# A long-convolution and token-MLP kernel: 16-bit table angles, three filter blocks evacuated by VectorE, the first filter half by column halves

## Chip, cores and metric

The kernel runs on one core of one Trainium2 chip. The metric is the device time of one execution in microseconds (us). Eleven runs of the kernel before had a median of 181.88 us (181.64 to 182.03). Names of engines in the profile are PE (TensorE), PEld (TensorE's weight loads), DVE (VectorE), ACT (ScalarE), POOL (GpSimd) and SP (SyncE, which only issues transfers here).

## The reference

Two branches of a mixer are computed on the same input and blended by a gate. Branch A convolves along the sequence (2048 positions, 640 channels) with a filter as long as the sequence; branch B is a layer norm and a two-layer MLP over the tokens.

```
x = A_q                                           # (1, 2048, 640)
g = sigmoid((x * gate_w).sum(-1))
# branch A
k_shift = sum over t<4 of k delayed by t, times shift_k
kv      = k_shift * v
y       = irfft(rfft(kv padded to 4096) * rfft(ssm_k padded to 4096))[:2048]
a       = x * (y + kv * ssm_D)
# branch B
h = layernorm(x)
u = gelu(einsum("bsd,sf->bdf", h, w1) + b1)       # w1: 2048 x 1536
b = (einsum("bdf,fs->bds", u, w2) + b2).transpose # w2: 1536 x 2048
out = g * a + (1 - g) * b
```

## The kernel before

**The work.** The convolution is done with transforms written as matmuls. A table FTB holds cosines and sines for four residues p = 0 to 3 of the position modulo 4 (128 partitions x 1024 values for each p). VectorE makes integer angles (`pint`), masks them to 4095, and ScalarE takes the sine of each block ("sin" in the source, `FTB<-pint,cst` in the profile). The filter `ssm_k` arrives with channels on partitions; TensorE transposes it by matmuls against an identity, in two halves h of the sequence and five blocks db of 128 channels (`transp`), and the transposed blocks are copied from PSUM to `wT`. The transforms of the filter (`fwd` for half 0, `fwd_even` and `fwd` for half 1, named "W") multiply `wT` by the table; ScalarE copies each result from PSUM to `C` ("We"). VectorE then mixes the four residues into spectra. The same is done for kv, the spectra are multiplied on VectorE, and the inverse transform runs on TensorE again. The MLP (`X`, `ring`, `GT`, `W2`) fills TensorE in between: matmuls "m1" of the first layer use the normalized `X`, those of the second layer, "m2", follow. VectorE takes the layer norm's statistics tile by tile (`ln_tile`, sixteen tiles of 128x640), POOL raises the variance to the power -0.5 (`ln_scale`, tile `rstd`), and VectorE normalizes in place (`ln_apply`), eight tiles at a time.

**Small parts at the start.** `zz` is a tile of zeros; TensorE multiplies it by itself in a few "spin" matmuls ahead of each transposed block of half 0 (`SPIN = (7, 3, 3, 2, 2)`). `ident` is the identity, made by VectorE out of POOL's `dif`. `rows` holds small constants that are rearranged by a VectorE copy ("taps") and transposed on TensorE into `cw`; POOL expands `cw` and the mask `m32` into `KF`, the weights of the four-tap shift. ssm_D is added to the filter's tap 0: its one row `Drow` is folded into the first transpose of every block of half 0 by an extra one-row matmul.

**What sets the order.** Every engine runs its instructions in the order in which they were issued. That order comes from a planner inside the kernel (`_Sched`), which at build time plays the instructions through with assumed costs (the second argument of `SC.add`, `dve_dur`, `act_dur`, or a `.dur` set by hand), picks the ready instruction with the smallest priority, and hands out four PSUM slots of two banks each (`pp0` to `pp3`; at most two to the MLP and three to the rest). A tracker (`_Tracker`) then adds the waits that data and buffers need. Planned times are only the planner's: on the chip the order is fixed, and the waits hold. Nearly all instructions are emitted by helpers, so one line of the profile stands for many: L295 is every matmul, L670 every ScalarE operation, L626 every `tensor_tensor`, L640 and L641 every `tensor_scalar`, L922 and L926 the statistics, L264 the transfers that add into their target, issued by POOL.

**Transfers.** SP issues the loads in program order: ssm blocks 0 and 1 to 2, then X's first quarter, then ssm blocks 3 to 4, the rest of X, biases, the second filter half, then w1, k and more.

Of the kernel before, what the change touches and what calls it, by code (L numbers as in the profile page):

```python
# [9 lines left out]
BF16 = mybir.dt.bfloat16  # L10
F32 = mybir.dt.float32
I32 = mybir.dt.int32
ACT = mybir.ActivationFunctionType
ALU = mybir.AluOpType

# [3 lines left out]
class _Tracker:  # L19
# [31 lines left out]
    def regions(self, ap):  # L51
        name = ap.tensor.name
        info = self.mem.get(name)
        if info is None:
            return []
        space, base, rowsize, esize = info
        apl = [tuple(p) for p in ap.ap]
        esz_ap = mybir.dt.size(ap.dtype)
        assert esz_ap == esize, "bitcast size change unsupported in tracker"
        off = ap.offset  # L60
        assert isinstance(off, int)
        pstride, pcount = apl[0]
        if pcount > 1:
            assert pstride == rowsize, (name, apl, rowsize)
        p0 = off // rowsize
        rem = off % rowsize
        p1 = p0 + pcount
        assert p1 <= 128
        free = apl[1:]
        outer = free[:-1]  # L70
        inner = free[-1:] if free else []
        nouter = 1
        for st, ct in outer:
            nouter *= ct
        res = []
        if outer and nouter <= 64:
            idxs = [0] * len(outer)
            for _ in range(nouter):
                o = rem
                for (st, ct), i in zip(outer, idxs):  # L80
                    o += st * i
                lo = o
                hi = o
                for st, ct in inner:
                    ext = st * (ct - 1)
                    if ext < 0:
                        lo += ext
                    else:
                        hi += ext
                hi += 1  # L90
                assert lo >= 0 and hi <= rowsize, (name, apl, off, rowsize)
                res.append(self._reg(space, p0, p1, base + lo * esize, base + hi * esize))
                for d in range(len(outer) - 1, -1, -1):
                    idxs[d] += 1
                    if idxs[d] < outer[d][1]:
                        break
                    idxs[d] = 0
        else:
            lo = rem
            hi = rem  # L100
            for st, ct in free:
                ext = st * (ct - 1)
                if ext < 0:
                    lo += ext
                else:
                    hi += ext
            hi += 1
            assert lo >= 0 and hi <= rowsize, (name, apl, off, rowsize)
            res.append(self._reg(space, p0, p1, base + lo * esize, base + hi * esize))
        return res  # L110
# [172 lines left out]
    def mm(self, ps_ap, lhsT, rhs, start, stop, final_val, inc, transpose=False):  # L283
# [8 lines left out]
                acc.append((r, "W"))  # L292
        need = self.deps_for("PE", acc)
        self.do_waits("PE", need)
        ins = self.nc.tensor.matmul(ps_ap, lhsT=lhsT, rhs=rhs, start=start, stop=stop, skip_group_check=True)  # L295
        src = ("eng", "PE", final_val)
        for reg, mode in acc_r:
            self.add_record(reg, "R", src)
# [213 lines left out]
def _build(nc, A_q, A_k, A_v, A_shift_k, A_ssm_k, A_ssm_D, B_x, B_w1, B_b1, B_w2, B_b2, gate_w, out):  # L512
# [6 lines left out]
    SL = 4 * D  # L519
# [3 lines left out]
    with ExitStack() as es:  # L523
# [58 lines left out]
        C = [alloc(f"C{i}", [128, 4, 4, D], BF16) for i in range(4)]  # L582
        SS = alloc("SS", [128, 2, 4, D], BF16)
        E_base = cur[0]
        acol = alloc("acol", [128, 2, 4], I32, at=base_of(SS))
        brow = alloc("brow", [128, 2, 128], I32, at=base_of(SS) + 64)
        dif = alloc("dif", [128, 128], I32, at=base_of(SS) + 64 + 1024)
        dif2 = alloc("dif2", [128, 32], I32, at=base_of(SS) + 64 + 1536)
        KT = [alloc(f"KT{i}", [128, NG, KTW], BF16) for i in range(2)]
# [4 lines left out]
        v1 = alloc("v1", [128, 2, 4, D], BF16, at=base_of(C[3]) + 2 * SL * 2)  # L594
        kv1 = alloc("kv1", [128, 2, 4, D], BF16, at=E_base)
        ksh = [alloc(f"ksh{i}", [128, 4, D], BF16, at=base_of(GT) + 5120 * (1 + i)) for i in range(2)]
        rows = alloc("rows", [20, 5, 512], BF16, at=base_of(GT))
        kn = [alloc(f"kn{i}", [128, 4, D], BF16, at=base_of(ring[1]) + 5120 * i) for i in range(2)]
        kp = [alloc("kp0", [128, NG, 128], BF16, at=base_of(ring[1]) + 10240), alloc("kp1", [128, NG, 128], BF16, at=base_of(GTB))]
        pint = alloc("pint", [128, 4, 2, 2, 256], I32, at=base_of(ring[1]))  # L600
        W2 = alloc("W2", [128, 32, 512], BF16, at=base_of(ring[0]))
        assert base_of(ring[1]) == base_of(ring[0]) + 16384
        O1 = alloc("O1", [128, 4, 4, D], BF16, at=base_of(X))
# [161 lines left out]

        SSM0 = ((0, 1), (1, 3), (3, 5))
        SSM1 = ((0, 2), (2, 5))
        small(Drow[:, :], dr(A_ssm_D, 0, [[0, 1], [1, D]]), 1280, "QA")
        small(rows[0:20, 0, 0:128], dr(A_shift_k, 0, [[128, 20], [1, 128]]), 5120, "QA")
        for a, b in SSM0[:2]:  # L770
            ssm_load(0, a, b)
        x_load(0)
        ssm_load(0, *SSM0[2])
        for hk in range(1, 4):
            x_load(hk)
        small(rows[0:4, 1, :], dr(B_b2, 0, [[512, 4], [1, 512]]), 4096, "SP", chain=True)
# [8 lines left out]
        SPIN = (7, 3, 3, 2, 2)  # L785

        def spin(k):
            return [((lambda s: s[:, 0:512]), zz[:, 0:128], zz[:, :], True, True)] * k

        T_PI = float(np.float32(math.pi * (1.0 - 1e-6)))  # L790
        memset("DVE", cst[:, 0:1], T_PI)
        memset("DVE", cst[:, 1:2], -0.5)
        iota = lambda ap, pat, b, cm: SC.add("POOL", 0.2, lambda s: T.op("POOL", lambda e: e.iota(ap, pat, base=b, channel_multiplier=cm), [], [ap]), [], [ap])
        iota(dif[:, :], [[1, 128]], 0, -1)
        iota(acol[:, :, :], [[4, 2], [1, 4]], 0, 8)
        iota(brow[:, :, :], [[-512, 2], [4, 128]], 1, 0)
        iota(dif2[:, :], [[1, 32]], 128, -1)
        ts("DVE", ident[:, :], dif[:, :], 0.0, None, ALU.is_equal)
        memset("POOL", rows[0:20, 3:5, :].rearrange("g a b -> g (a b)")[:, 0:896], 0.0)
        ro, ri = V(rows, 1536, [[128, 4], [160, 4], [1, 32]], pn=20), V(rows, 0, [[1, 4], [0, 4], [4, 32]], pn=20)  # L800
        SC.add("DVE", 0.6, lambda s: T.op("DVE", lambda e: e.tensor_copy(ro, ri), [ri], [ro]), [ri], [ro], prio=0, name="taps")
        PORD = (0, 2, 1, 3)
        sins = {}
        for p in PORD:
            pv = pint[:, p, :, 1, :]
            t_ = tt("DVE", pv, V(acol, p, [[4, 2], [0, 256]]), V(brow, 0, [[0, 2], [1, 256]]), ALU.mult, mode=1)
            ts("DVE", pint[:, p, :, 0, :], pv, 1024.0, None, ALU.add, mode=2)
            pa = pint[:, p, :, :, :].rearrange("q a b c -> q (a b c)")
            if p != 0:
                t_.after.add(pprev)  # L810
            pprev = ts("DVE", pa, pa, 4095, None, ALU.bitwise_and, mode=2)
            pv3 = pa
            sins[p] = act(FTB[:, p, :, :, :, :].rearrange("q a b c d -> q (a b c d)"), pa, ACT.Sin, bias=cst[:, 0:1],
                scale=-(2.0 * math.pi / 4096.0) * (1.0 - 1e-6), name="sin")

        for hk in range(2):
            k_load(hk)
# [14 lines left out]
        def consts():  # L832
# [5 lines left out]
            mms(vt, items, name="cst")  # L838
            act(cc[:, :], lambda s: s[:, 0:28], ACT.Copy, vt=vt, name="cc")

        def transp(h, db):
            vt = _VT("cv")
            items = []
            for kt in range(2):
                for p in range(4):
                    o = (lambda s, j=4 * kt + p: s[:, 128 * j:128 * j + 128])
                    dfold = h == 0 and kt == 0 and p == 0
                    if dfold:
                        items.append((o, ident[0:1, :], Drow[0:1, 128 * db:128 * db + 128], True, False))
                    items.append((o, V(ssm, db * S + 1024 * h + 4 * kt + p, [[8, 128]]), ident[:, :], not dfold, True))  # L850
            m_ = mms(vt, (spin(SPIN[db]) if h == 0 else []) + items, name="wtr")
            m_.dur = 0.5
            o_ = act(V(wT, 2 * h * SL + 128 * db, [[SL, 2], [D, 4], [1, 128]]), (lambda s: s[:, :].rearrange("q (a b c) -> q a b c", a=2, b=4)), ACT.Copy, vt=vt, name="wT")
            if h == 0:
                o_.after.add(sins[0 if db == 0 else 2])

        def fwd(src, h, p, dst, slot, scale, name, neg=lambda c, k2: False):
            for k2 in range(2):
# [80 lines left out]
                o_.after.update(lnlast[-1:])  # L939

        MIXP = 330
        LNA = 8
        lnlast = []
        kfirst = []
        KFP = (0, 5, 10, 15)
        srcW = lambda h: (lambda kt, p, ci: wT[:, 2 * h + kt, p, 320 * ci:320 * ci + 320])
        for h in range(2):
            for db in range(ND):
# [2 lines left out]
                consts()  # L951
            if h in (1,):
                fwd_even(srcW(h), h, C[h], 1.0 / 1024.0, h == 1, "W")
            for p in (PORD if h not in (1,) else PORD[2:]):
                if h == 0 and p in (1, 3):
                    sins[p].prio = SC.ops[-1].idx - (16.5 if p == 1 else 8.5)
                fwd(srcW(h), h, p, C[h], p, 1.0 / 1024.0, "W", (lambda c, k2: False) if h == 0 else (lambda c, k2: c == 1))
            if h == 0:
                for t in range(8):
# [11 lines left out]
                ln_apply(LNA, 16)  # L971
                lnlast.append(SC.ops[-1])
                for g0 in KFP:
                    tt("POOL", KF[:, g0:g0 + 20 // len(KFP), :, :], V(cw, 7 * g0, [[7, 20 // len(KFP)], [1, 7], [0, 32]]), V(m32, 0, [[0, 20 // len(KFP)], [0, 7], [1, 32]]), ALU.mult, xr=[pv3] if g0 == 0 else []).after.update(kfirst[:1])
                    kfirst.append(SC.ops[-1])
                for hk in range(2):
                    k_turn(hk)
# [341 lines left out]
```

## Time and profile before

| what | value |
|---|---|
| median of 11 runs | 181.88 us (181.64 to 182.03) |
| the profiled execution | 181.97 us, of which the profile's span covers 180.1 us |
| PE busy | 173.9 us, 97% of the span |
| DVE busy | 171.3 us, 95% |
| ACT busy | 117.0 us, 65% |
| POOL busy | 43.7 us, 24% |
| chain that ended last | PE 88%, ACT 10% |
| mean DMA rate | 242 GB/s |

The page gives the busy share of each engine, and the chain that ended last says which of them decided in each stretch. Spin matmuls on `zz` count as busy PE, so that the busy share of PE contains them. A start time is counted from the first instruction of the profile. Two instructions in a row on one engine can overlap by some tens of nanoseconds, so durations add up to a little more than the time they take together.

### The profile page before, as it was taken

The page shows a single profiled execution, that of the slowest core. Times are in us where ns is not written, and L with a number is a line of the kernel's source. Part 1 is how long each engine was busy: PE and PEld are TensorE (multiplying, and loading weights), DVE is VectorE, ACT ScalarE, POOL GpSimd, SP SyncE. Part 2 cuts the span into 40 slices and gives each one's busy share as a digit, 9 for nine tenths or more (in the row PEclk, how much of TensorE's full clock was granted, in tenths as well). Part 3 has the DMA queues.
Part 4 walks back from the last instruction along what each step waited for, and adds up shares of the span by engine and source line. Part 5 has one row for each costly group of instructions (what it writes and reads, how often), then busy time and mean ns, then how long its engine had stood idle before and what let it go on. Part 6 is the DMA issues. An engine that isn't in the chain of part 4 may idle for free.

```text
span 180.1 us, 3335 instructions
## 1 busy us (share of the span) xinstructions
PE 173.9 (97%) x1381; PEld 129.2 (72%) x1381; DVE 171.3 (95%) x203; ACT 117.0 (65%) x176; POOL 43.7 (24%) x42
## 2 busy tenths in 40 slices
PE   7979998989999999999999999999999999999994
PEld 2646785577779677776677778888888887777772
DVE  7999895999999999999999899999999999999984
ACT  5798998899898999616999933132131223753760
POOL 4079504090000054100240110402626000252000
PEclk9999999999999999999999999999999999999999
DMA  5999999999999999998399969798899999599563
GB/s 152 371 411 374 386 292 188 236 420 338 202 255 299 187 277 251 237 219 197 56 240 305 203 80 361 181 214 273 155 196 218 207 201 380 225 151 241 118 228 140
DMA packets 38543, 43.51 MB, mean 242 GB/s; under 512 B 15868, under 2 KB 31361, under 8 KB 38529
## 3 DMA queue, kind: packets, MB, share of 16 engines
q1 hardware_dynamic: 33296, 32.16, 58.1%
q0 software_dynamic: 5200, 11.14, 35.5%
q8 instruction: 11, 0.18, 0.4%
q14 instruction: 4, 0.02, 0.0%
q10 hardware_dynamic: 32, 0.01, 0.0%
HBM read 25.87 MB, written 2.62 MB: 158 GB/s over the span
## 4 chain that ended last, share of the span: by engine, by line
PE 88%; ACT 10%; DVE 0%; issue 0%
PE pp L295 88%; ACT wT L670 3%; ACT C L670 2%; ACT ksh L670 2%; ACT FTB L670 2%; ACT L670 1%; ACT GT L670 0%; DVE O L682 0%; DVE zz L686 0%; ACT cw L670 0%; DVE cst L686 0%
## 5 line engine op out<-in xcount | busy, mean ns | idle before, releaser
L295 PE MATMUL pp<-X,ring 128*128 128x320 bf16 x384 | 55.6, 299 | 0.0
L626 DVE TENSOR_TENSOR C<-C 128x2560 bf16<-128x2560 bf16 (+2 forms) x37 | 54.5, 1522 | 0.0
L295 PE MATMUL pp<-GT,W 128*128 128x320 bf16 x384 | 52.6, 299 | 0.0
L295 PEld LDWEIGHTS pp<-GT,W 128*128 128x128 bf16 x384 | 43.6, 114 | 8.6
L295 PEld LDWEIGHTS pp<-X,ring 128*128 128x128 bf16 x384 | 37.2, 98 | 14.7 <-DVE X L641 0.4
L670 ACT ACTIVATE C<-pp 128x640 bf16<-128x640 f32 x64 | 40.4, 723 | 4.8 <-PE pp L295 4.8
L670 ACT ACTIVATE O<-pp,c,omg 128x640 bf16<-128x640 f32 x15 | 13.3, 885 | 34.7 <-PE pp L295 34.7
L264 POOL DMA_DIRECT2D C<-C x8 | 10.9, 1611 | 41.7 <-DVE C L626 38.3
L295 PE MATMUL pp<-wT,FTB 128*128 128x320 bf16 x112 | 17.2, 299 | 2.1 <-ACT wT L670 1.0
L670 ACT ACTIVATE cgb<-pp,gg 128x640 bf16<-128x640 f32 x16 | 12.7, 794 | 5.7 <-PE pp L295 5.3
L295 PEld LDWEIGHTS pp<-wT,FTB 128*128 128x128 bf16 x112 | 10.5, 98 | 7.4 <-ACT wT L670 1.5
L670 ACT ACTIVATE GT<-pp,cc 128x640 bf16<-128x640 f32 x12 | 9.6, 800 | 9.0 <-PE pp L295 9.0
L626 DVE TENSOR_TENSOR tm<-C,C 128x2560 bf16<-128x2560 bf16 (+1 forms) x7 | 14.3, 2057 | 0.0
L922 DVE BATCH_NORM_STATS2 stats<-X 128x6 f32<-128x320 bf16 x32 | 13.6, 462 | 0.3 <-DMA X<-in_A_q_dram 0.3
L295 PE MATMUL pp<-C,FTB 128*128 128x320 bf16 x96 | 13.4, 299 | 0.0
L264 POOL DMA_DIRECT2D C<-q_hi x6 | 5.9, 977 | 27.7 <-DVE C L626 13.2
L295 PEld LDWEIGHTS pp<-C,FTB 128*128 128x128 bf16 x96 | 9.3, 98 | 3.8 <-issue 0.2
L670 ACT ACTIVATE gq<-gq 128x640 bf16<-128x640 bf16 x16 | 11.8, 741 | 0.0
L626 DVE TENSOR_TENSOR SS<-C 128x2560 bf16<-128x2560 bf16 x8 | 11.7, 1489 | 0.1
L626 DVE TENSOR_TENSOR C<-tm 128x2560 bf16<-128x2560 bf16 (+1 forms) x9 | 10.7, 1193 | 0.1
L670 ACT ACTIVATE wT<-pp 128x1024 bf16<-128x1024 f32 x10 | 9.7, 1040 | 1.0 <-PE pp L295 1.0
L670 ACT ACTIVATE ksh<-pp 128x1024 bf16<-128x1024 f32 (+1 forms) x12 | 9.8, 894 | 0.6 <-PE pp L295 0.6
(73 smaller groups left out, 194.8 us busy)
## 6 DMA issues: line engine op xcount, KB each, us to landing
ring<-in_B_w_dram SPq DMA_DIRECT2D x12, 512.0 KB, 7.7
W<-in_B_w_dram SPq DMA_DIRECT2D x12, 512.0 KB, 6.4
C<-C POOLq DMA_DIRECT2D x8, 640.0 KB, 10.6
X<-in_A_q_dram SPq DMA_DIRECT2D x4, 640.0 KB, 8.9
kn<-in_A_k_dram SPq DMA_DIRECT2D x4, 640.0 KB, 9.4
out_dram<-O SPq DMA_DIRECT2D x7, 320.0 KB, 3.4
C<-SS POOLq DMA_DIRECT2D x3, 640.0 KB, 11.7
ssm<-in_A_ssm_k_dram SPq DMA_DIRECT2D x3, 512.0 KB, 7.3
```

What stands on the lines that cost most here:

```text
L264: ins = engobj.dma_start(out_ap, in_ap, accum_op=ALU.add, max_dma_last_dim=2560)
L295: ins = self.nc.tensor.matmul(ps_ap, lhsT=lhsT, rhs=rhs, start=start, stop=stop, skip_group_check=True)
L626: o_ = SC.add(eng, d, lambda s: T.op(eng, lambda e: e.tensor_tensor(o, a, b, op), rd, [o]), rd, [o], prio=prio, name="tt")
L670: return T.op("ACT", lambda e: e.activation(o, src, func, **kw), rr + [src], ww)
L922: ops.append(SC.add("DVE", 0.38, (lambda o, i: lambda s: T.op("DVE", lambda e: e.bn_stats(o, i), [i], [o]))(o, i), [i], [o]))
```

## The change

Five things are changed together.

1. **Angles in 16 bits.** One 128x128 product of partition and column index, masked to 4095, is kept as a 16-bit table `tb` (with its copy shifted by 1024). POOL writes eight 16-bit rows `jrow` of offsets. Each block's angles are one 16-bit sum of the two and one 16-bit mask, in place of a 32-bit product, a 32-bit sum over half the block and a 32-bit mask. `pint` shrinks to 16 bits.
2. **Transposes in bf16.** The transposes write bf16 into PSUM (`is_transpose`), 2 KB for each block instead of 4 KB, and the spin matmuls write into the slot's other bank. Blocks 0 to 2 of half 0 are copied to `wT` by VectorE (`evac_dve`), the rest by ScalarE as before.
3. **ssm_D by columns.** ssm_D is loaded as five rows of 128, transposed once by TensorE (`dcol`), copied by VectorE to `Dc` and added into the loaded filter by three small VectorE operations (`addD`). The one-row matmuls go.
4. **The first filter half by column halves.** `fwd_c` runs all four residues for columns 0 to 319, which need blocks 0 to 2, and then all four for columns 320 to 639. It has the same number of matmuls and evacuations as `fwd`.
5. **Loads and small orders.** All three ssm loads of half 0 come ahead of X. The zeroing of `rows` goes from POOL to VectorE; `ident` follows the table; the taps copy follows the angles; `KF` waits for `wT` of block 2 instead of for the last angles; the hand-set priorities of two sines go.

```diff
-        iota(dif[:, :], [[1, 128]], 0, -1)
-        iota(acol[:, :, :], [[4, 2], [1, 4]], 0, 8)
-        iota(brow[:, :, :], [[-512, 2], [4, 128]], 1, 0)
+        PORD = (0, 2, 1, 3)
+        iota(brow[:, :], [[4, 128]], 1, 0)
+        iota(acol[:, :], [[0, 1]], 0, 8)
+        jr = lambda p, kt: iota(jrow[:, 2 * p + kt, :], [[-512 * (4 * kt + p), 2], [4 * (4 * kt + p), 128]], 4096 + 4 * kt + p, 0)
...
-        memset("POOL", rows[0:20, 3:5, :].rearrange("g a b -> g (a b)")[:, 0:896], 0.0)
+        tt("DVE", prod[:, :], V(acol, 0, [[0, 128]]), brow[:, :], ALU.mult, mode=1)
+        tbv, pr16 = tb[:, 1, :, :], prod[:, :].bitcast(I16).rearrange("q (m t) -> q t m", t=2)[:, 0:1, :].broadcast_to([128, 2, 128])
+        SC.add("DVE", 0.25, lambda s: T.op("DVE", lambda e: e.tensor_scalar(tbv, pr16, 4095, None, op0=ALU.bitwise_and), [prod[:, :]], [tbv]), [prod[:, :]], [tbv])
+        ts("DVE", tb[:, 0, :, :], tb[:, 1, :, :], 1024.0, None, ALU.add, mode=2)
+        memset("DVE", rows[0:20, 3:5, :].rearrange("g a b -> g (a b)")[:, 0:896], 0.0)
...
-            pv = pint[:, p, :, 1, :]
-            t_ = tt("DVE", pv, V(acol, p, [[4, 2], [0, 256]]), V(brow, 0, [[0, 2], [1, 256]]), ALU.mult, mode=1)
-            ts("DVE", pint[:, p, :, 0, :], pv, 1024.0, None, ALU.add, mode=2)
+            pv = V(pint, 1024 * p, [[512, 2], [256, 2], [1, 256]])
+            t_ = tt("DVE", pv, V(tb, 0, [[0, 2], [256, 2], [1, 256]]), V(jrow, 512 * p, [[256, 2], [0, 2], [1, 256]]), ALU.add)
...
+        def dcol():
+            vt = _VT("cv")
+            mms(vt, [((lambda s: s[:, 0:5]), Dr5[:, :], ident[0:5, 0:5], True, True)], prio=0, name="dcol")
+            evac_dve(Dc[:, :], (lambda s: s[:, 0:5]), vt, prio=0)
...
+        def addD(a, b):
+            o = V(ssm, a * S, [[S, b - a], [1, 1]])
+            stt("DVE", o, o, 1.0, V(Dc, a, [[1, b - a], [1, 1]]), ALU.mult, ALU.add, prio=0)
...
+            if (h, db) in WTD:
+                o_ = evac_dve(o, i, vt, prio=0)
+                o_.dur = 0.62
+            else:
+                o_ = act(o, i, ACT.Copy, vt=vt, name="wT")
...
+        def fwd_c(p, ci, dst, scale):
+            for k2 in range(2):
+                vt = _VT("cv")
+                items = []
+                for kt in range(2):
+                    for c in range(2):
+                        items.append((chk(c), FTB[:, p, kt, c, k2, :], srcW(0)(kt, p, ci), kt == 0, kt == 1))
+                m_ = mms(vt, (spin(WSPIN) if (p, ci, k2) == (0, 0, 0) else []) + items, name="W")
+                m_.dur = 0.54
+                act(V(dst, p * SL + k2 * D + 320 * ci, [[2 * D, 2], [1, 320]]), two, ACT.Copy, vt=vt, name="We", scale=scale)
...
+        WTD = ((0, 0), (0, 1), (0, 2))
+        WSPIN = 3
...
-                    tt("POOL", KF[:, g0:g0 + 20 // len(KFP), :, :], V(cw, 7 * g0, [[7, 20 // len(KFP)], [1, 7], [0, 32]]), V(m32, 0, [[0, 20 // len(KFP)], [0, 7], [1, 32]]), ALU.mult, xr=[pv3] if g0 == 0 else []).after.update(kfirst[:1])
+                    tt("POOL", KF[:, g0:g0 + 20 // len(KFP), :, :], V(cw, 7 * g0, [[7, 20 // len(KFP)], [1, 7], [0, 32]]), V(m32, 0, [[0, 20 // len(KFP)], [0, 7], [1, 32]]), ALU.mult, xr=[V(wT, 256, [[1, 128]])] if g0 == 0 else []).after.update(kfirst[:1])
```

## The prediction

> **What bounds the kernel now.** I read the chain of waits first, since it says which engine ends each stretch last.
>
> ```profile
> 1.18 4.40 PE pp L295 x16
> 5.58 0.02 issue
> 5.60 1.02 ACT wT L670
> 6.63 2.08 ACT FTB L670 x2
> 8.70 0.91 ACT wT L670
> ...
> 11.74 1.84 ACT wT L670 x2
> 13.58 0.05 issue
> 13.63 16.40 PE pp L295 x142
> ...
> 41.31 136.12 PE pp L295 x1048
> ```
>
> The columns are start, length and piece. From 5.6 to 13.6 us ScalarE decides: five filter evacuations (wT) and three of the four sines (FTB) in one queue. The change attacks that stretch. From 13.63 on it is TensorE almost to the end. But VectorE is 95% busy too, so I asked for busy time by stretch; the columns are window, length, then busy time of PE, weight load, DVE, ACT and POOL.
>
> ```profile
> 33.30:60.00 26.70, 25.90 (x282) 19.71 (x281) 26.37 (x22) 25.21 (x37) 4.98 (x1) 1.00 1.09 292
> 60.00:90.00 30.00, 30.00 (x228) 21.34 (x226) 30.00 (x24) 22.96 (x44) 6.30 (x5) 1.00 0.89 204
> 90.00:120.00 30.00, 30.00 (x223) 23.05 (x222) 29.04 (x32) 18.12 (x33) 5.86 (x6) 1.00 0.98 225
> 120.00:150.00 30.00, 30.00 (x223) 25.06 (x222) 29.69 (x18) 7.96 (x9) 7.33 (x6) 1.00 1.01 215
> 150.00:169.40 19.40, 19.40 (x144) 14.52 (x143) 19.33 (x17) 11.25 (x14) 4.80 (x4) 1.00 0.88 237
> ```
>
> Between 33.3 and 169.4 VectorE is busy 134.43 of 136.10 us, so it has only 1.67 us to give. The timeline shows that TensorE leans on it: the second half's inverse matmuls start at 165.30 on C, whose sum (the first of a pair that starts at 163.66, 1.49 long) ends at 165.15, and at 169.64 on SS, whose pair ends at 169.48. Two engines are thus in step to 0.2 us, and whatever starts VectorE's long stream late ends the kernel late, though the chain names TensorE alone. That stream starts here (timeline; brackets hold the idle time before, and its releaser):
>
> ```profile
> 8.20 0.49 DVE L922 BATCH_NORM_STATS2 stats<-X 128x6 f32<-128x320 bf16 x1 [0.30 <-DMA X<-in_A_q_dram]
> ...
> 19.55 0.21 DVE L926 BATCH_NORM_AGGREGATE mv<-stats 128x2 f32<-128x12 f32 x1
> 20.32 2.94 DVE L641 TENSOR_SCALAR X<-X,mv,rstd 128x640 bf16<-128x640 bf16 x8 [0.57 <-POOL rstd L626]
> ...
> 30.45 2.94 DVE L641 TENSOR_SCALAR X<-X,mv,rstd 128x640 bf16<-128x640 bf16 x8 [2.11 <-POOL rstd L626]
> ```
>
> Statistics of twelve tiles, then the first normalization at 20.32. Only the 0.57 there can absorb lateness: the 2.11 is VectorE waiting for POOL's answer to its own last statistic, and moves with it.
>
> [...] No VectorE copy from PSUM is in the trace; the nearest row is the final 128x320 f32 operation, 0.552 us[...]. [...] The bf16 rows agree: 1280 elements 0.821, 2560 elements 1.487 (0.52 ns each); the int16 forms are not in the trace. [...] the seven spin matmuls from 1.18 span 3.17 (0.43 each), the three from 7.35 span 0.81 (0.22 each). [...]
>
> **The change, part by part**, following the order of instructions that the changed program is built with.
>
> *Angles.* Before, each of four blocks costs VectorE 0.684 + 0.424 + 0.690. After: a product of 128 ([...]0.29), two table operations (0.42 strided, 0.22), the memset of rows moved from POOL (448 words; zz's 256 take 0.272: 0.47), then per block an add of 1024 int16 (0.69) and a mask (0.42). Four blocks fall from 7.2 to 4.4, but 1.4 of setup comes ahead of the first. ident moves behind it. With 0.08 of overlap between independent neighbours: ident ends at 2.85, the first mask at 3.9, so the first sine starts at 3.95, not 3.43. POOL's eight jrow tables cost 0.3 each (brow's row: 0.338 for 256) and keep ahead: the pair for the first add is there at 1.8. Its dif2 and memset move behind them, to about 3.5; they have slack.
>
> *TensorE's start.* The fold of D left the transposes (five 0.22 us matmuls gone) and became a column: one matmul (dcol), a 0.2 us copy (Dc) and three tiny adds of about 0.17. But dcol is TensorE's first instruction and waits for ident: 2.9 us, where spinning began at 1.18. Behind it stand seven spins at half clock, 2.99, and then the transposes of block 0, which end at 6.8 instead of 5.6. VectorE, ready for that block's evacuation at 5.7, waits until 6.93: **1.25 idle**, with everything on its queue behind it, masks for two sines included.
>
> *Evacuations.* Three wT copies leave ScalarE (3 x 1.02) and enter VectorE (3 x 0.72). Walking on: wT0 6.93 to 7.65, taps to 7.98, dif2, add and m32 to 8.3, mask 1 to 8.65, angle add 3 to 9.26. The taps matmuls on TensorE now wait for taps, so three spins (0.65) and block 1's eight transposes (0.5) end at 9.35; wT1 9.52 to 10.24; again spins and transposes, wT2 10.67 to 11.39; the last add; mask 3 to 11.8. **Statistics start at 11.74.** Twelve tiles at 0.858 (seven take 6.01 from 13.07) plus 0.2 end at 22.25, against 19.76.
>
> *POOL.* KF now waits for wT2 instead of the last angle: 11.45 to 19.6 (8.13 busy), rstd ready at 21.7. That is before 22.25, so the old 0.57 is absorbed. The first normalization moves from 20.32 to 22.25: **+1.93**.
>
> *ScalarE.* The last sine runs 11.86 to 13.0, then wT3 and wT4 to 15.06, and filter evacuations start at 15.0, not 14.24 (+0.7). The split by column halves keeps 16 groups of four matmuls and 16 evacuations at 0.61; one group runs before block 3 arrives, but its result waits for ScalarE: worth nothing while that queue is late.
>
> *DMA.* On SP's queue the third ssm load passes the first X load. Each lands within what it replaces: X moves from 8.15 to about 9.5 (512 KB took 1.3), hidden under statistics that start at 11.7; exposed it would cost 1.3. The kn loads wait for the last sine, +1.25, hidden by a DMA queue that is nine tenths full; exposed, up to 1.3 on the kp copies. ACT's queue loads D as five rows instead of one, issued at 0.72 and needed at 2.9; nothing in the trace waits for the old form, and if it landed later than 2.9 it would delay dcol by as much. POOL's queue keeps its order.
>
> *Sum.* +1.93 into a stream with 1.67 of slack, of which 0.8 (a wait for ScalarE's tanh) might give; against that the first vkv product needs ksh, which I reckon up to 0.9 late because TensorE's half-1 groups come in one run paced by two PSUM slots. I let these cancel: +2.0 on the profiled execution's 181.97, 0.09 above the median of 181.88. **Forecast 183.9 us.**
>
> **Rivals.**
> *Slower still.* TensorE stays at half clock[...]: spins 1.28, transposes 0.86 per block, statistics at 14.06, +4.2: 186.1.[...] For it: late TensorE start, a gap of 1.2 us before taps. Against: a 2.99 us run of spins and more following.
> *No change.* The new waits on VectorE do not occur: the clock opens early and transposes land by 5.7. Without its 1.9 us of waits statistics start at 9.8 and end at 20.3, where the old start was 20.32: 181.9. Or the int16 and bf16 forms buy nothing and the change does not do what it says; that ends in the slower case instead.
> *Faster.* ScalarE's relief reaches the end. If mask 3 is done by 9.9, the last sine ends at 11.1 and filter evacuations start at 13.1, 1.1 early; TensorE then runs ahead. It decides if statistics start by 9.8 and the 1.67 of VectorE idle gives way: 180.8. Against it: VectorE's queue gained about 1.3 us of work (10.3 against 9.0) and lost none later.
>
> **How the numbers follow.** A measurement of this kernel tells 0.2% (0.36 us) from no change. Main case 0.53 (own range 183.0 to 184.9); slower still 0.32; no change 0.06; faster 0.09. So slower 0.85, same 0.06, faster 0.09. The range 181.8 to 186.0 leaves out most of the faster case and the far end of the half-clock one.
>
> **What would show it.** In the changed profile: dcol near 2.9; a VectorE wait for TensorE ahead of the first wT copy of about 1.2;[...] statistics from 11.7; first normalization at 22.2 with no wait for rstd; filter evacuations from 15.0; TensorE's inverse starting some 2 us later. The forecast is wrong if normalization is not late, or if it is late and TensorE's inverse is not.

## The result, and the profile after

The changed kernel takes **185.13 us** (median of 12 runs, 183.78 to 186.13), against 181.88 before: ratio **1.0169, 95% interval 1.0148 to 1.019**. The median stands between two groups and is the time of neither: six runs lie at 183.78 to 184.30, six at 185.96 to 186.13. The profiled execution took 186.04 us and is of the upper group; its span is 183.8 us (before: 180.1).

The chain of waits of the changed kernel (start, length, piece):

```profile
2.75 4.13 PE pp L298 x16
6.88 0.02 issue
6.90 0.69 DVE wT L684
7.59 0.33 DVE rows L829
7.92 0.05 issue
7.97 4.52 PE pp L298 x29
12.49 0.02 issue
12.51 0.69 DVE wT L684
...
24.00 2.54 DVE X L649 x7
...
36.01 142.16 PE pp L298 x1144
```

ScalarE's queue of evacuations and sines, which filled 5.6 to 13.6 us of the chain before, is gone from it. In its place TensorE and VectorE alternate; ScalarE decides later, from 15.02 to 19.36. TensorE starts at 2.75 instead of 1.18, and VectorE's copies of the turned blocks wait for it. The timeline of the same stretch (brackets: idle time of the engine before it, and the releaser):

```profile
2.75 0.16 PE L298 MATMUL pp<-ident,Dr 5*128 5x5 bf16 x1 [2.75 <-DVE ident L648]
2.84 3.17 PE L298 MATMUL pp<-zz 128*128 128x512 bf16 x7
5.80 1.06 PE L298 MATMUL pp<-ident,ssm 128*128 128x128 bf16 x8
6.90 0.69 DVE L684 COPY wT<-pp 128x1024 bf16<-128x1024 bf16 x1 [1.45 <-PE pp L298]
8.25 1.46 PE L298 MATMUL pp<-zz 128*128 128x512 bf16 x3
9.51 1.06 PE L298 MATMUL pp<-ident,ssm 128*128 128x128 bf16 x8
10.60 0.69 DVE L684 COPY wT<-pp 128x1024 bf16<-128x1024 bf16 x1 [1.46 <-PE pp L298]
12.31 0.81 PE L298 MATMUL pp<-zz 128*128 128x512 bf16 x3
12.51 0.69 DVE L684 COPY wT<-pp 128x1024 bf16<-128x1024 bf16 x1 [1.22 <-PE pp L298]
13.52 1.27 DVE L968 BATCH_NORM_STATS2 stats<-X 128x6 f32<-128x320 bf16 x3
24.00 2.54 DVE L649 TENSOR_SCALAR X<-X,mv,rstd 128x640 bf16<-128x640 bf16 x7
```

Read the lengths of the spin matmuls (`zz`). Three of them take 1.46 us from 8.25 and 0.81 from 12.31. The clock opened between those two groups: the trace records it at 12.06 us, where the kernel before had it from 6.46. Until then three spins take 1.46 us instead of 0.81, and a block's eight transposes 1.06 where they take 0.66 after 14 us. VectorE loses 1.45 + 1.46 + 1.22 = 4.13 us ahead of the three copies. The statistics, queued behind them, start at 13.52 (before: 8.20) and the first normalization at 24.00 (20.32), without a wait for rstd.

VectorE is as full as before once it is under way. By stretch (window, length, busy time of PE, weight load, DVE, ACT, POOL):

```profile
60.00:90.00 30.00, 30.00 (x238) 21.37 (x236) 30.00 (x23) 24.21 (x44) 5.10 (x4) 1.00 0.95 204
...
120.00:150.00 30.00, 30.00 (x223) 25.09 (x221) 29.62 (x18) 8.56 (x10) 7.33 (x6) 1.00 1.01 211
```

So its lateness is carried to the end, where the timeline shows one thing more:

```profile
169.30 4.51 PE L298 MATMUL pp<-C,FTB 128*128 128x320 bf16 x32
169.67 2.89 DVE L634 TENSOR_TENSOR SS<-C 128x2560 bf16<-128x2560 bf16 x2
173.65 4.51 PE L298 MATMUL pp<-SS,FTB 128*128 128x320 bf16 x32
177.99 1.79 PE L298 MATMUL pp<-GT,W 128*128 128x320 bf16 x12
```

The same stretch of the kernel before:

```profile
165.30 4.51 PE L295 MATMUL pp<-C,FTB 128*128 128x320 bf16 x32
166.59 2.89 DVE L626 TENSOR_TENSOR SS<-C 128x2560 bf16<-128x2560 bf16 x2
169.64 4.51 PE L295 MATMUL pp<-SS,FTB 128*128 128x320 bf16 x32
173.99 3.42 PE L295 MATMUL pp<-GT,W 128*128 128x320 bf16 x24
```

Before, VectorE's last pair on SS started at 166.59 and TensorE read it at 169.64, 3.05 later: the pair's 2.89 and a handover. Now the pair starts 3.08 later, at 169.67, but TensorE reads it 3.98 after that, since it is still busy with the transforms on C. And only 12 products of the last output tile (GT, W) follow, where 24 did. The planner, given other instructions at the start, has moved 12 of them ahead of the last inverse transforms.

These two times, the start of VectorE's last SS pair and TensorE's first read of SS, are my measure for every run below. From that read to the end of the span it is 10.46 us before and 10.15 after. Hence the span's 3.7 us are 3.08 (VectorE later) + 0.93 (TensorE's order at the end) - 0.31 (a shorter rest). A further 0.35 us lies outside the span, where the profile shows nothing: the profiled execution is 186.04 - 183.82 = 2.22 us longer than its span, against 181.97 - 180.10 = 1.87 before.

### The profile page after: what moved, and what is told of

Its sections match the earlier page's. It is cut to its first block, busy times and chain, and to the rows that moved or that the text cites. A ratio compares the mean times of both kernels' runs of the same rounds, so it can differ in the third digit from the quotient of the medians.

```text
span 183.8 us, 3336 instructions
## 1 busy us (share of the span) xinstructions
PE 174.1 (95%) x1377; PEld 129.6 (71%) x1377; DVE 171.5 (93%) x210; ACT 114.5 (62%) x173; POOL 46.8 (25%) x49
## 4 chain that ended last, share of the span: by engine, by line
PE 85%; DVE 8%; ACT 3%; POOL 1%; issue 1%; DVEq 0%; POOLq 0%
PE pp L298 85%; DVE X L649 3%; DVE stats L968 2%; ACT C L678 1%; ACT wT L678 1%; POOL rstd L634 1%; DVE kp L759 1%; DVE wT L684 1%; DVE cgb L634 0%; ACT cgb L678 0%; DVE O L690 0%; DVE mv L972 0%; DVE O L634 0%; DVEq L508 0%; DVE rows L694 0%
## 5 line engine op out<-in xcount | busy, mean ns | idle before, releaser
L678 ACT ACTIVATE O<-pp,c,omg 128x640 bf16<-128x640 f32 x15 | 13.3, 884 | 33.7 <-PE pp L298 33.7
L298 PE MATMUL pp<-wT,FTB 128*128 128x320 bf16 x112 | 17.7, 300 | 1.7 <-ACT C L678 0.9
L298 PEld LDWEIGHTS pp<-wT,FTB 128*128 128x128 bf16 x112 | 9.9, 98 | 8.3 <-ACT C L678 3.8
L968 DVE BATCH_NORM_STATS2 stats<-X 128x6 f32<-128x320 bf16 x32 | 13.6, 465 | 0.0
L634 POOL TENSOR_TENSOR KF<-cw,m 128x1120 bf16<-128x1120 bf16 x4 | 8.2, 2088 | 8.9 <-DVE ssm L658 8.9
L267 POOL DMA_DIRECT2D O<-q_hi x4 | 4.8, 1200 | 21.3 <-DVE q_hi L634 21.3
```

The costliest lines, as they stand in the source:

```text
L267: ins = engobj.dma_start(out_ap, in_ap, accum_op=ALU.add, max_dma_last_dim=2560)
L634: o_ = SC.add(eng, d, lambda s: T.op(eng, lambda e: e.tensor_tensor(o, a, b, op), rd, [o]), rd, [o], prio=prio, name="tt")
L678: return T.op("ACT", lambda e: e.activation(o, src, func, **kw), rr + [src], ww)
L968: ops.append(SC.add("DVE", 0.38, (lambda o, i: lambda s: T.op("DVE", lambda e: e.bn_stats(o, i), [i], [o]))(o, i), [i], [o]))
```

## The experiments

My theory after the result was that TensorE's late start and its warming matmuls, at half clock, delay VectorE, and that VectorE's stream sets the end. The rivals were the work added to VectorE, the column halves, the angles, and transfers. All times below are medians; the kernel before took 181.9 to 182.0 us beside these runs. The last three columns are of one profiled execution; those of after (the changed kernel), e1, e6 and p4 are among the slowest of their kernel.

| run | median us | ratio to before, 95% interval | VectorE's last SS pair | TensorE reads SS | span |
|---|---|---|---|---|---|
| before | 181.88 | | 166.59 | 169.64 | 180.1 |
| after | 185.13 | 1.0148 to 1.019 | 169.67 | 173.65 | 183.8 |
| e1_spin_first | 183.73 | 1.0064 to 1.0138 | 168.31 | 172.29 | 182.5 |
| e2_spin_first_only | 182.79 | 1.0025 to 1.0061 | 166.55 | 170.28 | 180.5 |
| e8_no_spins | 182.81 | 1.004 to 1.0069 | 166.29 | 170.27 | 180.5 |
| e3_late_start_before | 183.63 | 1.0072 to 1.0106 | 167.80 | 170.86 | 181.3 |
| e4_angles_before | 183.25 | 1.0051 to 1.0083 | 167.62 | 170.68 | 181.1 |
| e9_angles_only | 182.51 | 1.0015 to 1.0036 | 166.84 | 169.90 | 180.4 |
| e5_scalar_copies | 183.85 | 1.0076 to 1.0139 | 167.40 | 171.63 | 181.8 |
| e6_residue_order | 185.76 | 1.0158 to 1.0235 | 168.82 | 173.72 | 183.9 |
| p0_before | 181.85 | 0.9979 to 1.0006 | 166.48 | 169.54 | 180.0 |
| p2_no_spins | 182.96 | 1.0047 to 1.0092 | 166.29 | 170.26 | 180.4 |
| p3_tail | 182.22 | 1.0006 to 1.0038 | 166.31 | 169.36 | 179.8 |
| p4_tail_split | 185.58 | 1.0149 to 1.0229 | 169.09 | 173.82 | 184.3 |

TensorE reads SS 3.05 to 3.06 us after the start of VectorE's pair wherever the end of its order is that of the kernel before (before, e3, e4, e9, p0, p3), and 3.73 to 4.90 after it in the other runs.

In e1, e3 and e8 every engine's order is otherwise that of the kernel each is compared with. In e4, e5, e6, e9 and p4 the planner also orders later instructions differently, so that these runs compare the named part together with a new order.

### Spins moved, taken out, and a late start alone

**e1_spin_first** is the changed kernel with the seven first spins ahead of the column of D, so that TensorE starts at 1.18 again:

```diff
-            mms(vt, [((lambda s: s[:, 0:5]), Dr5[:, :], ident[0:5, 0:5], True, True)], prio=0, name="dcol")
+            mms(vt, spin(SPIN[0]) + [((lambda s: s[:, 0:5]), Dr5[:, :], ident[0:5, 0:5], True, True)], prio=0, name="dcol").dur = 0.06
...
-            m_ = mms(vt, (spin(SPIN[db]) if h == 0 else []) + items, name="wtr")
+            m_ = mms(vt, (spin(SPIN[db]) if h == 0 and db > 0 else []) + items, name="wtr")
```

> Only TensorE's order differs from the changed kernel: its seven spin matmuls come ahead of dcol instead of behind it, so that TensorE starts near 1.2 us and not at 2.75. Theory A (TensorE's late start delays the transposes, keeps the half clock, and thereby holds VectorE's queue): first wT copy at about 5.7 with no wait, clock open by 6.5 to 8, statistics from 10.5 to 11.3, first normalization near 21 to 21.7, and 182.5 to 183.2 us with a narrow spread. Theory B (the loss is the 1.3 us of work that VectorE gained, and the late start is hidden): no more than 0.5 us below the changed kernel's faster runs, 183.6 or more. Theory C (the column halves and ScalarE's later evacuations set it): about 185 as the changed kernel, whatever TensorE's start.

Measured: 183.73 us, 1.4 us of the 3.25 given back. That is above theory A's range and just inside theory B's. The wait ahead of the first copy is gone (it starts at 5.58). The waits ahead of the second and third (1.46 and 1.18) stay, and so do two groups of times, 183.02 to 183.08 and 184.39 to 184.87. In its profile, of the upper group, the clock opened at 10.64, so that the early start alone did not open it early.

**e2_spin_first_only** also takes out all later spins:

```diff
-        SPIN = (7, 3, 3, 2, 2)
+        SPIN = (7, 0, 0, 0, 0)
...
-        WSPIN = 3
+        WSPIN = 0
```

> As the run with the spins first, and the later spins (3, 3, 3, 2, 2) are gone too. Theory A: each pair of spin groups that stands on the way to a VectorE copy is worth up to 0.65, so statistics start at 9.5 to 9.9, first normalization 20.0 to 20.4 as in the kernel before, filter evacuations by ScalarE at 12.6 to 12.9 (before 14.24); 181.3 to 182.0 us. If instead the clock shuts for want of spins, TensorE takes 0.86 per block and 1.1 per filter group and the time is 184 or more. Theory B: 183 or more in any case.

Measured: 182.79 us (182.46 to 183.05), between the ranges of both theories. No copy waits for TensorE any more, although the clock, open from 4.53, shut again from 7.94 to 14.77 (granted over the whole profile: 0.976).

**e8_no_spins** is the changed kernel with no spin at all (`SPIN = (0, 0, 0, 0, 0)`, `WSPIN = 0`).

> This is the changed kernel (185.1 us, in two groups near 184.1 and 186.0) without any warming matmul: TensorE's first work is the column of D at 2.75 us. Theory that the warming matmuls, issued at half clock, are what delays the turned blocks, and with them VectorE: as in e2_spin_first_only, 182.6 to 183.0 us and no two groups over 1 us apart. Theory that the clock has to be opened by these matmuls: the transposes and the first transforms then run at half clock, 20 of them by 0.13 us and more later, and the time stays at 185 to 187 us.

Measured: 182.81 us. Of 22 runs, 18 lie within 182.69 to 182.91; the other four are scattered up to 184.81. The two groups 1.9 us apart are gone, as the first theory said. A small split is left: the four scattered runs have spans of 180.9 to 181.0 us and a granted clock of 0.995, the others 180.4 to 180.7 and 0.999 to 1.0. Its timeline:

```profile
2.74 0.16 PE L298 MATMUL pp<-ident,Dr 5*128 5x5 bf16 x1 [2.74 <-DVE ident L648]
3.87 1.36 PE L298 MATMUL pp<-ident,ssm 128*128 128x128 bf16 x8 [0.97 <-DMA ssm<-in_A_ssm_k_dram]
7.84 0.69 DVE L684 COPY wT<-pp 128x1024 bf16<-128x1024 bf16 x1 [0.22 <-PE pp L298]
8.69 0.69 DVE L684 COPY wT<-pp 128x1024 bf16<-128x1024 bf16 x1 [0.16 <-PE pp L298]
9.53 1.22 PE L298 MATMUL pp<-wT,FTB 128*128 128x320 bf16 x4 [0.88 <-DVE ssm L658]
10.37 1.28 DVE L968 BATCH_NORM_STATS2 stats<-X 128x6 f32<-128x320 bf16 x3 [0.58 <-DMA X<-in_A_q_dram]
```

The late start at 2.74 is still there, but here it costs next to nothing by itself: the first transposes wait for the filter's landing at 3.87 anyway. Here the clock did not open until 13.34, so transposes and the first transforms ran at half clock throughout (sixteen transposes from 6.73 took 1.93 us, where sixteen took 1.22 in the changed kernel at 24.96), and still VectorE's waits for blocks shrank from 4.13 to 0.38. The warming matmuls cost more than the warmth was worth in the stretch that they were to serve. With them gone the next limit shows: the statistics wait 0.58 for X, whose first load now stands behind the third filter load.

**e3_late_start_before** does the opposite to the kernel before: a small product of ident and m32 ahead of its spins, so that TensorE starts at 2.88.

```diff
+            gate = [((lambda s: s[:, 0:32]), ident[:, :], m32[:, :], True, True)] if h == 0 and db == 0 else []
-            m_ = mms(vt, (spin(SPIN[db]) if h == 0 else []) + items, name="wtr")
+            m_ = mms(vt, gate + (spin(SPIN[db]) if h == 0 else []) + items, name="wtr")
```

> The kernel before, with one matmul of ident and m32 put ahead of its first spins, so that TensorE starts at about 2.85 instead of 1.18; nothing else moves. It computes nothing that is used. Theory A for TensorE alone: first wT evacuation at about 7.0 instead of 5.6, later clock opening[...], ScalarE's chain 1.3 to 2.5 late, and the end late by about as much: 183.0 to 184.5, perhaps in two groups of times. If a late start is hidden by later slack: 181.9.

Measured: 183.63 us, 1.7 more than its 181.97 beside it, with the angles, the copies and the halves of the kernel before. Its first copy starts at 6.96 instead of 5.60, the filter transforms at 14.98 instead of 13.63, VectorE's last SS pair 1.21 later. Spins behind a late first instruction are thus enough for a loss of this size. Here the transposes did not run at half clock (block 0's eight took 0.71, as those of later blocks did), and the six times lie within 0.41 us.

### The parts beside the spins

**e4_angles_before** is the kernel before with the 16-bit angles alone (the lines of `tb`, `jrow` and `pint` as in the change; zeros of `rows` still by POOL; `KF` no longer waits for the last angles).

> The kernel before with the 16-bit angles alone (product table, jrow rows by POOL, 16-bit sum and mask; KF then waits for cw and m32 only). VectorE's opening gets some 1.3 us shorter, statistics run without interruption from 8.2. Theory A: the first normalization still waits for POOL's rstd (KF, then the power) until about 20.1 to 20.3, and ScalarE's queue of evacuations and sines is unchanged, so 181.6 to 182.0: no difference. Rival: the gain reaches the end, 180.8 or less; or POOL's eight more tables hold up what follows, 182.5 or more.

Measured: 183.25 us, slower, but for the larger part not for the angles' own sake. Its timeline:

```profile
1.90 0.98 POOL L690 MEMSET rows<- 20x896 bf16 x1
2.14 2.01 DVE L644 TENSOR_SCALAR tb<-tb 128x256 int16<-128x256 int16 x1
2.85 1.84 POOL L797 IOTA jrow<- 128x256 int16 x6
```

A table operation that takes 0.30 us in the changed kernel took 2.01 beside POOL's memset, and the first sine started at 5.37 instead of 3.43. That the memset was the cause was my guess; **e9_angles_only** tests it by taking the memset off POOL:

```diff
-                memset("POOL", rows[0:20, 3:5, :].rearrange("g a b -> g (a b)")[:, 0:896], 0.0)
...
+        memset("DVE", rows[0:20, 3:5, :].rearrange("g a b -> g (a b)")[:, 0:896], 0.0)
```

> This is the kernel before with the 16-bit angles alone, like e4_angles_before (183.25 us), but with the zeros of rows written by VectorE as the changed kernel does, so that POOL has no memset beside the table operations. Theory that e4's 2.02 us operation came from that memset: it takes 0.30 us here, the first sine starts near 3.5. Theory that the angles' saving on VectorE (5.3 us of angle work instead of 6.9) goes into the time: 180.7 us. Theory that POOL's KF and rstd set the first normalization whatever VectorE saves: first normalization near 20.3, second near 30.5, 181.7 to 182.3 us.

Measured: 182.51 us, 0.2 above the range that I gave. The table operation took 0.30 and the first sine started at 3.88. So the length goes with the memset; the operation also stood beside `jrow` tables in both runs, without harm in this one. What made it so long is not shown: in e4 it began at 2.14, 0.24 after the memset, and ended at 4.15, 1.27 after the memset had ended. Of e4's loss, 0.74 us goes with the memset. The other 0.6 (182.51 against 181.90 beside it) stays with the angles and their order, and the saving on VectorE brought nothing:

```profile
20.04 2.94 DVE L645 TENSOR_SCALAR X<-X,mv,rstd 128x640 bf16<-128x640 bf16 x8 [1.27 <-POOL rstd L630]
```

The first normalization starts 0.28 earlier than before, having waited 1.27 for rstd instead of 0.57: POOL, with KF (8.14 us from 9.88, before 8.13 from 10.17) and the power, ends only that much earlier. VectorE's last pair is even 0.25 later, of which a new 0.26 wait for C is the only sign that I found. Why this kernel is slower stays open.

**e5_scalar_copies** is e2_spin_first_only with the three copies back on ScalarE (`WTD = ()`).

> This is e2_spin_first_only with the three copies of the turned filter blocks 0 to 2 back on ScalarE. Its partner measured 182.8 us. VectorE gets back 3 x 0.69 = 2.07 us, ScalarE gets 3 copies more of about 0.97 us. Theory that VectorE's added copies are the cost: about 180.7 us. Theory that ahead of 45 us VectorE is held by others anyway (by POOL, whose KF products of 8.2 us and rstd of 2 us end near 19.5, and by ksh, which comes off ScalarE at 40.8): the 2.07 us turn into waits for rstd in front of the first normalization, ScalarE's 3 us make ksh later by 0.5 to 2.5 us, and the time is 183.2 us (182.8 to 184.8).

Measured: 183.85 us, 1.1 slower than e2. Its timeline:

```profile
11.25 8.13 POOL L634 TENSOR_TENSOR KF<-cw,m 128x1120 bf16<-128x1120 bf16 x4 [6.75 <-ACT wT L678]
21.41 2.59 DVE L649 TENSOR_SCALAR X<-X,mv,rstd 128x640 bf16<-128x640 bf16 x7 [2.03 <-POOL rstd L634]
```

VectorE's 2.07 us of copies became 2.03 us of waiting. I had put the loss in ksh; it is in POOL. KF is made to wait for block 2, which ScalarE copies later than VectorE did (KF starts at 11.25, in e2 at 9.18), and rstd stands behind KF. So giving the copies back to ScalarE gains nothing as long as KF waits for block 2. The run does not show what VectorE's added copies would cost if KF were free to start.

**e6_residue_order** is e2_spin_first_only with `fwd` in place of the column halves.

> This is e2_spin_first_only (182.8 us) with the first filter half transformed residue by residue, as in the kernel before, instead of by column halves; the first transform then needs all five blocks and starts near 13.2 instead of 9.2 us. Theory that the start of TensorE's transforms bounds the opening: 2 to 4 us slower, 185 us or more. Theory that VectorE's stream and the chain to ksh through ScalarE set the end: nothing on VectorE ahead of 30 us changes, ksh comes 0 to 0.8 us later, 182.8 to 183.6 us. Theory that the column halves themselves cost (their order of evacuations): 182.0 us or less.

Measured: 185.76 us, 3.0 slower than e2 and in the first theory's range. Its timeline:

```profile
13.05 4.43 PE L298 MATMUL pp<-wT,FTB 128*128 128x320 bf16 x19 [2.29 <-ACT wT L678]
36.70 3.63 DVE L634 TENSOR_TENSOR C<-C 128x1280 bf16<-128x1280 bf16 x3 [0.97 <-ACT C L678]
41.12 1.49 DVE L634 TENSOR_TENSOR vkv<-ksh,vkv 128x2560 bf16<-128x2560 bf16 x1 [0.79 <-ACT ksh L678]
```

TensorE waits 2.29 us for the fifth block, then finds the clock shut from 13.57 to 16.98 (19 products of 0.23 each; granted over the profile: 0.991). ScalarE gets its results late, and VectorE waits for C and ksh. The column halves, which start these transforms at 9.17 in e2, are therefore a help once TensorE is not behind with spins. But the 3.0 us are not theirs alone. In this profile (186.35 us, 0.6 above the median) VectorE's last pair is 2.27 later than in e2, and TensorE's read of SS another 1.17, since the planner has put 52 products of the last tiles (7.23 us) ahead of the transforms on C, where e2 has 44 (6.14 us). How much of the 2.27 is the shut clock, this run does not tell.

### The end of TensorE's order

e8 leaves a riddle: VectorE's last pair starts 0.30 earlier than before, and the chain of waits leaves TensorE at 174.80 instead of 177.43, yet the time is 0.9 longer. Some 0.4 of that is in the span (medians 180.4 and 180.0) and is looked for here; the other 0.4 is outside (time less span: 2.36 in e8, 1.96 in the kernel before beside it). The next runs replace the eight transposing DMAs (KT from kp, GTB from FTB) by plain copies, `dma_start` for `dma_start_transpose`, so that they leave these transpositions out, and are compared with each other. **p0_before** is the kernel before with this edit, **p2_no_spins** is e8 with it.

> This is the kernel before with its eight transposing DMAs (KT from kp, GTB from FTB) made plain copies of the same bytes: it leaves those two transpositions out and is the base for the runs named p. The copies free the SP queue sooner (a transposing issue held it 3.4 us) and land sooner, but KT was ready 3 to 4 us ahead of its first use in e8_no_spins. Theory that VectorE's stream and TensorE's products set the end: as the kernel before, 181.6 to 182.1 us. Theory that the transfers' landings are on the path: 1 us or more faster.

> This is e8_no_spins (the changed kernel without warming matmuls, 182.8 us) with the same two transpositions left out as in p0_before. As e8_no_spins against the kernel before, 0.9 us slower than p0_before: 182.5 to 183.1 us; if the landings were what made the difference between the two, within 0.3 us of p0_before.

Measured: 181.85 and 182.96 us, each as its partner with transpositions (181.88 and 182.81). The difference between the two is not made by those transfers.

**p3_tail** adds to p2 an edge that holds back the last tile's first half until the last inverse transform is planned:

```diff
+                        lastm2.append(SC.ops[-1])
...
-                    mms(vt, items, name="inv")
+                    invs.append(mms(vt, items, name="inv"))
...
         inverse(1, Z1)
+        lastm2[0].after.add(invs[-1])
```

> This is p2_no_spins (transpositions left out) with one thing changed in TensorE's order: all 24 products of the last output tile (GT, W) stand behind the last inverse transforms (SS), as they do in the kernel before, instead of 12 ahead of them. In e8_no_spins VectorE hands over SS at 169.2 us, 0.3 earlier than in the kernel before, but TensorE reads it at 170.3, 0.6 later, because it has 12 products of 0.135 us more ahead of it. Theory that this order takes back what the opening brought: TensorE reads SS 0.6 to 1.0 us earlier, and the time falls by as much, to 181.6 to 182.3 us. Theory that the order at the end is only the mark of a VectorE that is late: as p2_no_spins within 0.2 us.

Measured: 182.22 us, 0.74 less than p2, inside the first theory's range. The order of the other instructions is the same in both. Timeline of p2, then of p3:

```profile
165.91 4.51 PE L298 MATMUL pp<-C,FTB 128*128 128x320 bf16 x32
170.26 4.51 PE L298 MATMUL pp<-SS,FTB 128*128 128x320 bf16 x32
174.61 1.79 PE L298 MATMUL pp<-GT,W 128*128 128x320 bf16 x12
```

```profile
165.02 4.51 PE L298 MATMUL pp<-C,FTB 128*128 128x320 bf16 x32 [0.56 <-DVE C L634]
169.36 4.51 PE L298 MATMUL pp<-SS,FTB 128*128 128x320 bf16 x32
173.71 3.42 PE L298 MATMUL pp<-GT,W 128*128 128x320 bf16 x24
```

With the 12 products behind it, the transform on C can start 0.89 earlier, and now it waits 0.56 for VectorE: that wait shows VectorE setting the end, which the gapless TensorE of the other runs had hidden. What is left against the kernel before is 0.2% (ratio 1.0006 to 1.0038), and it lies outside the span: p3's median span is 179.8 us, under the 180.0 of p0, but its time is 2.34 longer than its span, p0's 1.94. What takes that time these runs do not show.

**p4_tail_split** tried for a version faster than both, by computing the second normalization's 1/sigma in two parts (`ln_scale(LNA, 12)` early, `ln_scale(12, 16)` late).

> This is p3_tail (transpositions left out) with the second normalization's 1/sigma computed in two parts: that of tiles 8 to 11 already beside the first normalization, that of tiles 12 to 15 after it. In e8_no_spins VectorE idles 2.1 us ahead of the second normalization. Theory that any idle time of VectorE ahead of 45 us goes into the time: the wait shrinks to 0.7 us or less and the time is 180.4 to 181.2 us, under both kernels. Theory that ksh, which comes off ScalarE at 39.9 us, bounds VectorE next: its wait ahead of the v-k product grows from 0.3 to 1.5 us or more, and the time stays within 0.5 us of p3_tail.

Measured: 185.58 us, and neither theory was tested. The wait for rstd is gone, but the planner now orders VectorE's opening otherwise: a kp copy is placed where its load has not landed (1.30), two C sums wait for ScalarE (1.23 and 0.93), and the wait for ksh is 1.44. The times again fall in two groups, three runs at 184.25 to 184.72 with a granted clock of 1.0 and three at 186.43 to 186.68 with 0.991. In the profile, of the upper group, TensorE waits 2.10 us for C at the end, since the 24 products that could fill the gap stand behind it, as in p3; the clock then shuts from 168.60 to 172.01, and the transforms on C take 6.18 us instead of 4.51. Whether VectorE's 2.1 us ahead of the second normalization can be had stays open. No run here beat the kernel before.

## Why the prediction was right, and where it was not

- **Direction and size.** Forecast 183.9, range 181.8 to 186.0; measured 185.13. The main case (183.0 to 184.9) is the lower group of runs, near 184.1. The "slower still" rival, TensorE at half clock, is the upper one: 186.1 forecast, 186.0 measured. I gave one or the other; the kernel does both. That the groups differ by the time at which the clock opens is not shown, since no run near 184.1 has a profile. The granted clocks speak for it. In the profiles of the changed kernel and of e1 the clock opens once and shuts 170.67 us later, near the end; the run's granted clock then falls short of 1 by half the share of the time after that (in the changed kernel 1.10 of 183.82 us, and the granted clock was 0.997). If it was so in the other runs of the changed kernel, their spans and granted clocks (0.995 to 0.997) give an estimated opening at 9.1 to 10.2 us in the six faster runs and 11.4 to 12.0 in the six slower, give or take 0.2.
- **Luck in the size.** Both numbers fit better than the terms behind them. The rival's +4.2 was all VectorE's lateness; the profile has 3.08 of that, and 0.62 of TensorE's order (0.93 less the shorter rest) and 0.35 outside the span, both of which I had at nothing. If the last two are the same in the lower group, its 2.2 us over the kernel before hold an estimated 1.2 of VectorE's lateness, where the main case had about 2.
- **The late start.** dcol near 2.9 (2.75), transposes of block 0 to 6.8 (6.86), VectorE's wait 1.25 (1.45): right. That spins, behind a late start and at half clock, cause most of the loss is shown by e3 on the one side and by e1 and e8 on the other: taking them out gives back 2.3 of the 3.25 us.
- **Second and third block.** I put wT1 at 9.52 and wT2 at 10.67, with a warm TensorE; they came at 10.60 and 12.51. This is the step that failed for the upper group: 1.8 us of half clock. The half-clock rival had statistics at 14.06 (13.52). With the masks queued behind the copies the last sine came at 13.64 (11.86 forecast) and the first filter evacuation at 16.87 (15.0).
- **The later stages.** POOL's rstd was to come in time for a first normalization at 22.25: there was no wait, at 24.00. Of that 3.68 us of lateness 0.6 was made up by VectorE's last SS pair; of the 1.67 of slack I had thought that 0.8 might give. I let it cancel against ksh; ksh's new wait was 0.57 where I had "up to 0.9". **The missing term** is TensorE's order at the end: +0.93 at SS in the profile, 0.62 with the shorter rest behind it; undoing it took 0.74 us off the median (p3 against p2). The prediction does not follow TensorE's order to its end.
- **Column halves "worth nothing while that queue is late".** In the changed kernel as it stands no run tests that; in e2, where the queue is not late, they are worth at most the 2.27 us by which VectorE is later in e6's profile.
- **The X load.** Hidden, as said; with the spins gone it is exposed by 0.58 of the 1.3 that I had priced (e8).
- **The rivals.** "No change" asked for statistics at 9.8 and gave 181.9; e2 had them at 9.35 and took 182.79, because of the order at the end (SS read 0.64 later than before) and of some 0.4 us outside the span. "Faster" asked for the same and gave 180.8; in e2 a new wait of 1.06 for ksh took the lead of 0.45 that VectorE still had at its second normalization.
- **Prices.** The trace before shows no copy from PSUM by VectorE and no int16 form; what I put in for them were estimates. The copy from PSUM took 0.69 (0.72 put in); the int16 sum took 0.68 (0.69) and the mask 0.43 (0.42). One table operation took 0.31, not 0.42, the other 0.30, not 0.22. ident took 0.23, where it took 0.45 before.

## What to carry to other kernels

Warming matmuls are work in TensorE's queue: in front of an instruction that others wait for, and at half clock, they can cost more than they bring, so look first at whether that stretch needs the clock at all (e8 did not have it before 13.3 us and is 2.3 us faster than the changed kernel). When a planner orders the program, compare its order to the very end: a change in the first 10 us moved 12 matmuls at 165 us, and putting them back was worth 0.74 us. And where TensorE shows no gap, ask what it is filled with; a gapless engine can be the one that is waiting, on work that could have stood later.

## What the runs showed of the hardware

- **In three profiles the changes of the clock lie 3.41 us apart, or twice that.** In e6 its record changes at 10.16, 13.57 and 16.98 us, 3.41 apart both times; in e2 at 4.53, 7.94 and 14.77, 3.41 and 6.83 apart; in p4 at 168.60 and 172.01.
- **After the same seven spins the clock opened at different times.** In the kernel before and in e2 they took 3.17 us from 1.18, and the clock opened at 6.46 and at 4.53; it opened at 5.80 in p0, at 10.64 in e1 and at 12.06 in the changed kernel, where they start at 2.84. Why it opened when it did is not shown. The two groups of the changed kernel lie 1.9 us, 1.0%, apart; if the estimate above holds, that is because VectorE waits for the cold part (1.46 and 1.22 us ahead of its second and third copy in the profile). The times of the kernel before do not part into two groups.
- **A small VectorE operation of 0.30 us took 2.01** with a memset of 0.98 us running on POOL (e4), and 0.30 without it (e9). The part of the 2.01 that lies behind the memset's end is not explained.
- **A gap late in TensorE's work was followed by half clock.** In p4's profile a wait of 2.10 us at 165.70 is followed by 3.41 us of half clock from 168.60, and 32 products took 6.18 us instead of 4.51. In p3 a wait of 0.56 at the same place was not.
